# Six packed tiles in place of seven, pruning in nine pieces in place of six, and natural tiles 6 to 11 by column halves from two transposing loads

## Chip, cores, metric

One core of one Trainium2 chip. The metric is the device time of one execution in microseconds (us), median of several; the profile's own span is about 1.8 us shorter than that time. A run is called fast when it lies within 1.5% of the fastest run of the same kernel, otherwise slow. Only fast runs are compared, unless it is said otherwise; a single look has no state of its own.

## The reference

```python
# B, S, D = 16, 512, 1024; all bf16
wg = w.reshape(G, 4, D)                      # 2:4 sparsity along the rows of w
mag = jnp.abs(wg)
thr = ...                                    # second largest magnitude of each four
wp = (wg * (mag >= thr)).reshape(D, D)
return jnp.einsum("bsd,df->bsf", x, wp) + b  # 8192 tokens x 1024 x 1024
```

So: prune the weights, then a dense product of 8192 x 1024 by 1024 x 1024, which is 64 token tiles of 128.

## The kernel before

Pruning compares four rows of w, so w is loaded "packed": the four rows of a group lie side by side in a partition. A few token tiles (the packed tiles, 0 to 6) are multiplied in this packed order, with x transposed on the matrix engine (PE), while the rest of w is still being pruned piece by piece on VectorE. The pruned pieces are also saved to memory and loaded again in natural row order (`reload`). The remaining 57 tiles (natural tiles) use that copy, and x that a transposing load brings in.

```python
NPK = 7                                   # packed tiles
batches: 5, 4, 8, 8, ...                  # natural tiles of one transposing load each
pieces = [(0,0,256), (0,256,512), (1,0,256), (1,256,512), (0,512,1024), (1,512,1024)]
# (row half of w, called group 0 or 1; first column, last column); order of all PE, VectorE and ScalarE work is a fixed list:
#   T6a = transpose x of tile 6, group 0;  F5 = 5 filler matmuls (on zeros, unused);  M5.1 = tile 5 with piece 1;
#   abs/hi/lo/t1/t2/thr/mask/mult + piece = pruning;  C = copy a transpose out;  S = stage;
#   W4 = save piece 4 from ScalarE's queue
...
run(order)
save(0, 0, 256); save(0, 256, 512); save(1, 0, 256); save(1, 256, 512)    # SyncE's queue
load_batch(0)        # transposing load, 5 tiles
reload(0)            # columns 0..511 of the pruned weights, natural order, 1 MB
reload(1)            # columns 512..1023, needs the saves of pieces 4 and 5
load_batch(1)        # transposing load, 4 tiles
load_batch(2)
for t in (2, 0, 3, 1, 6, 5, 4):
    finish(t)        # bias, output store of a packed tile
# first batch of natural tiles: column half 0 of all its tiles, then half 1;
# all later tiles: both halves together
```

## Time and profile before

235.36 us, median of 3 runs (235.29 to 235.66).

| what | value | view |
|---|---|---|
| PE's share of the chain that ended last | 98% | the page, part 4 |
| first packed matmul / first natural matmul | 7.01 / 33.46 us | timeline of PE |
| last product of the pruning (VectorE) | 26.00 us | timeline of VectorE |
| last save landed | 32.15 us | semaphore events of the trace |
| second reload: issued, landed, wanted by PE | 32.22, 38.95, about 42.1 us | the same, and the timeline |

The chain that ended last, by engine and by line. L394 are the natural matmuls of both halves, L359 those by one half, L219 the packed ones, L131 fillers, L194 transposes:

```profile
PE 98%; DVE 0%; issue 0%
PE ps L394 76%; PE ps L219 10%; PE ps L359 9%; PE ps L131 2%; PE tp L194 2%; DVE o L363 0%; DVE zeros L80 0%
```

The last pieces of the same chain in order of time, up to 51 us (start, duration, what). There is no wait in it; packed work (L219) goes straight over into natural work (L359):

```profile
15.63 2.62 PE ps L219 x24
18.25 0.22 PE tp L194 x4
18.48 15.14 PE ps L219 x84
33.62 17.27 PE ps L359 x80
```

SyncE's queue in order of time (start, duration of the issue). The two reloads stand together; the issue of the second waits inside that row for the last save. The next transposing load (L244) comes after both:

```profile
17.45 5.87 SPq L244 DMA_TRANSPOSE xb<-in_x_dram  x1
23.50 9.10 SPq L184 DMA_DIRECT2D wp_nat<-wp_scratch  x2
32.64 25.50 SPq L244 DMA_TRANSPOSE xb<-in_x_dram  x2
```

The transfers (what, queue, count, KB each, us from issue to landing), first for the saves issued between 26 and 27 us, then for the reload issued at 32.2 us:

```profile
wp_scratch<-wp ACTq DMA_DIRECT2D x2, 512.0 KB, 5.2
...
wp_nat<-wp_scratch SPq DMA_DIRECT2D x1, 1024.0 KB, 6.7
```

### The profile page before, as it was taken

How to read it: one execution, taken by the hardware profiler on the slowest of the kernel's cores; microseconds unless marked ns; L12 is line 12 of the kernel's file. 1: busy time of each engine (PE TensorE's matmuls, PEld its weight loads, DVE VectorE, ACT ScalarE, POOL GpSimd, SP SyncE). 2: the span in 40 equal slices, each digit the busy share in tenths (PEclk: the TensorE clock that was granted, in tenths of full speed). 3: DMA queues.
4: the chain of work that ended last, by engine and by line, in shares of the span. 5: the costliest groups of instructions: out<-in, count | busy, mean ns of one | idle time of the engine just before them, and what ended most of it. 6: DMA issues, size and time to landing. Idle time of an engine off the chain costs nothing.

```text
span 233.2 us, 2871 instructions
## 1 busy us (share of the span) xinstructions
PE 229.5 (98%) x1184; PEld 112.8 (48%) x1184; DVE 104.2 (45%) x177; ACT 15.2 (7%) x27; POOL 0.7 (0%) x6
## 2 busy tenths in 40 slices
PE   8999999999999999999999999999999999999995
PEld 5987444444444444444444444444444444444443
DVE  3999559533343244244234334334324424423434
ACT  3679000000000000000000000000000000000000
POOL 1000000000000000000000000000000000000000
PEclk9999999999999999999999999999999999999999
DMA  6999969999999952992239921697221221122122
GB/s 189 297 327 248 322 214 224 282 257 247 241 340 258 273 166 88 209 285 94 90 74 253 257 91 46 146 239 202 90 90 49 88 93 63 72 90 91 47 89 90
DMA packets 79500, 40.29 MB, mean 173 GB/s; under 512 B 60416, under 2 KB 71936, under 8 KB 79488
## 3 DMA queue, kind: packets, MB, share of 16 engines
q1 hardware_dynamic: 68208, 22.32, 43.9%
q10 hardware_dynamic: 11280, 17.80, 22.9%
q8 instruction: 9, 0.15, 0.3%
q14 instruction: 3, 0.02, 0.0%
HBM read 6.29 MB, written 18.87 MB: 108 GB/s over the span
## 4 chain that ended last, share of the span: by engine, by line
PE 98%; DVE 0%; issue 0%
PE ps L394 76%; PE ps L219 10%; PE ps L359 9%; PE ps L131 2%; PE tp L194 2%; DVE o L363 0%; DVE zeros L80 0%
## 5 line engine op out<-in xcount | busy, mean ns | idle before, releaser
L394 PE MATMUL ps<-wp_nat,xb 128*128 128x512 bf16 x816 | 176.3, 379 | 0.0
L394 PEld LDWEIGHTS <-xb 128*128 128x128 bf16 x816 | 79.8, 98 | 96.3
L363 DVE TENSOR_TENSOR o<-ps,bias_sb 128x512 bf16<-128x512 f32 (+1 forms) x116 | 74.0, 677 | 117.2 <-PE ps L394 110.8
L219 PE MATMUL ps<-wp,xt 128*128 128x256 bf16 (+1 forms) x168 | 25.5, 308 | 0.0
L359 PE MATMUL ps<-wp_nat,xb 128*128 128x512 bf16 (+2 forms) x112 | 21.1, 349 | 0.0
L219 PEld LDWEIGHTS <-xt 128*128 128x128 bf16 x168 | 16.2, 98 | 7.5
L359 PEld LDWEIGHTS <-xb 128*128 128x128 bf16 x112 | 10.4, 98 | 10.7
L233 DVE TENSOR_TENSOR o<-ps,bias_sb 128x512 bf16<-128x512 f32 x7 | 4.8, 685 | 5.1 <-PE ps L219 5.1
L131 PE MATMUL ps<-zeros 128*128 128x128 bf16 (+1 forms) x32 | 5.3, 328 | 1.0 <-DVE zeros L80 1.0
L154 ACT ACTIVATE mag<-w_sb 128x1024 bf16<-128x1024 bf16 (+1 forms) x4 | 6.0, 1488 | 1.0 <-DMA w_sb<-in_w_dram 1.0
L151 DVE TENSOR_TENSOR wp<-w_sb,mag 128x1024 bf16<-128x1024 bf16 (+2 forms) x7 | 5.4, 766 | 0.2
L151 DVE TENSOR_TENSOR mag<-mag,hi 128x1024 bf16<-128x1024 bf16 (+2 forms) x7 | 5.3, 767 | 0.2
L199 ACT COPY xt<-tp 128x256 f32<-128x256 f32 x14 | 4.9, 372 | 5.3 <-PE tp L194 5.3
L194 PE MATMUL tp<-ident,x 128*128 128x128 bf16 x56 | 5.0, 227 | 0.0
L234 DVE TENSOR_TENSOR o<-st,bias_sb 128x512 bf16<-128x512 f32 x7 | 4.8, 679 | 0.0
L131 PEld LDWEIGHTS <-zeros 128*128 128x128 bf16 x32 | 3.0, 125 | 2.6 <-issue 1.7
L194 PEld LDWEIGHTS <-x 128*128 128x128 bf16 x56 | 4.0, 117 | 0.4 <-DMA x<-in_x_dram 0.2
L228 ACT COPY st<-ps 128x512 f32<-128x512 f32 x7 | 3.6, 609 | 0.1
L151 DVE TENSOR_TENSOR hi<-mag 128x512 bf16<-128x512 bf16 (+1 forms) x6 | 3.0, 507 | 0.0
L151 DVE TENSOR_TENSOR lo<-mag 128x512 bf16<-128x512 bf16 (+1 forms) x6 | 3.0, 508 | 0.0
L161 DVE TENSOR_SCALAR mag<-w_sb 128x1024 uint16<-128x1024 uint16 x2 | 0.9, 427 | 2.9 <-DMA w_sb<-in_w_dram 2.9
L151 DVE TENSOR_TENSOR hi<-hi,lo 128x256 bf16<-128x256 bf16 (+1 forms) x6 | 2.0, 336 | 0.2
(11 smaller groups left out, 6.4 us busy)
## 6 DMA issues: line engine op xcount, KB each, us to landing
out_dram<-o ACTq DMA_DIRECT2D x58, 256.0 KB, 3.9
wp_nat<-wp_scratch SPq DMA_DIRECT2D x2, 1024.0 KB, 6.4
x<-in_x_dram SPq DMA_DIRECT2D x5, 256.0 KB, 5.0
out_dram<-o ACTq DMA_DIRECT2D x10, 128.0 KB, 1.7
w_sb<-in_w_dram SPq DMA_DIRECT2D x4, 256.0 KB, 4.3
w_sb<-in_w_dram SPq DMA_DIRECT2D x2, 512.0 KB, 7.1
wp_scratch<-wp SPq DMA_DIRECT2D x4, 256.0 KB, 5.6
wp_scratch<-wp ACTq DMA_DIRECT2D x2, 512.0 KB, 5.2
```

Source lines behind the costliest of these rows:

```text
L131: pe(nc.tensor.matmul(warm_ps[:, :rep * P], lhsT=zeros[:], rhs=zeros[:, None, :].to_broadcast([P, rep, P]), start=True, stop=True))
L151: dve(nc.vector.tensor_tensor(out, a, b_, op=op))
L154: act(nc.scalar.activation(self.mag[:], self.w, Act.Abs))
L194: pe(nc.tensor.transpose(tp[:, m, :], xg[:, m, :], ident[:]))
L199: act(nc.scalar.copy(xt[:].bitcast(fp32), xpk[(t, g)][:].bitcast(fp32)))
L219: pe(nc.tensor.matmul(ps[:, c0 - h * FH:c1 - h * FH], lhsT=xpk[(t, g)][m], rhs=wp[:, g, m, c0:c1], start=(new and m == ms.start), stop=(le ...
L228: act(nc.scalar.copy(st[:], ps_open.pop((t, 0))[:]))
L233: dve(nc.vector.tensor_tensor(o[:, FH:], ps_open.pop((t, 1))[:], bias_sb[:, FH:], op=Alu.add))
L234: dve(nc.vector.tensor_tensor(o[:, :FH], staged.pop(t)[:], bias_sb[:, :FH], op=Alu.add))
L359: pe(nc.tensor.matmul(ps, lhsT=xt[:, kt, :], rhs=wp_nat[:, kt, c0:c1], start=(kt == 0), stop=(kt == KT - 1)))
L363: dve(nc.vector.tensor_tensor(o[:, c0:c1], ps, bias_sb[:, c0:c1], op=Alu.add))
L394: pe(nc.tensor.matmul(pss[h][:], lhsT=xt[:, kt, :], rhs=wp_nat[:, kt, h * FH:(h + 1) * FH], start=(kt == 0), stop=(kt == KT - 1)))
```

## The change

Its intent: start the packed matmuls earlier (a first piece of only 128 columns, with its own smaller load), hide VectorE's dependent gaps by interleaving the chains of neighbouring pieces, and save eight transposes with one packed tile fewer. PE then comes to the natural tiles one tile earlier, so six of them (6 to 11) are done by halves, to give the second reload time; their x comes in two loads of three tiles, the second one between the reloads.

```diff
-    NPK = 7
-    ... batches of 5, 4, 8, 8, ...
+    NPK = 6
+    for nb in (3, 3, 4, 8, 8, 8, 8, 8, 8): ...
+    LEAD = 2                                  # batches done by column halves
-    load_w(0, 0, 256)
+    load_w(0, 0, 128)
     ...
+    load_w(0, 128, 256)
     ...                                       # order of the other loads changed too
-    pieces = [(0, 0, 256), (0, 256, 512), (1, 0, 256), (1, 256, 512), (0, 512, 1024), (1, 512, 1024)]
+    pieces = [(0, 0, 128), (0, 128, 256), (0, 256, 512), (1, 0, 256), (1, 256, 512), (0, 512, 768), (0, 768, 1024), (1, 512, 768), (1, 768, 1024)]
     order = { ...                             # new lists for PE, VectorE, ScalarE
+            "T5a F12 T3a T2a F8 M5.0y M3.0y M5.1 M2.1 M2.0y T4a M3.1 M5.0x M2.0x T1a T0a ...
     ...
     load_batch(0)
     reload(0)
+    load_batch(1)
     reload(1)
-    load_batch(1)
     load_batch(2)
-    for t in (2, 0, 3, 1, 6, 5, 4):
+    for t in (3, 2, 1, 0, 4, 5):
         finish(t)
     ...                                       # column halves for all tiles of the first LEAD batches
```

## The prediction

> **What bounds the kernel.** The matrix engine (PE). The chain of waits is 98% PE: 76% in the paired natural matmuls, 9% in natural groups of one column half, 10% in packed matmuls, 2% fillers, 2% transposes. In the timeline PE starts at 0.99 us, never rests over 0.1 us, and ends at 230.5 of 233.2 us. Only PE work and new holes in PE's row can change the time.
>
> **PE work.** Start-to-start steps in the timeline: 216 ns for a 512-column natural matmul, 109 ns for a 256-column packed one, 107 ns for a 128-column filler or transpose until about 5.1 us and 56 ns after it. The Trainium skill, "TensorE: Matmul & The Clock Gate", Part 1, gives the same two steps for a cold and a warm array; this trace agrees.
> - Sixteen column-half matmuls go from packed (2 x 109 ns) to natural (216 ns): about -0.04 us.
> - The 256-column first piece becomes two of 128: estimated 56 ns a matmul instead of 54.5: +0.07 us.
> - Eight transposes fewer, two fillers more. Before, the first packed matmul starts at 7.01 us, behind 20 transposes and 18 fillers. After, it stands behind 12 and 20: I estimate 6.57 us if nothing waits. -0.4 us.
> Net: -0.35 to -0.4 us of 235.36. The change trims only the start.
>
> **Can pruning feed PE that early?** VectorE's rule in the timeline: duration about 0.15 us + 0.53 ns an element; an independent instruction starts 0.08 us before its predecessor ends, a dependent one 0.03 us after. That reproduces the pruning of before to 0.03 us (last product 26.0 us). Applied to the new order: 22 more VectorE instructions, but interleaving hides most dependent gaps. The first load is half the size; I estimate it lands at 3.4 us (before: 3.77), the first product is ready at 6.4, the last at 26.8 us. PE needs nearly each piece just as it comes: I estimate 0 to 0.4 us of holes, typically 0.1, mostly near 7.8 us. Its 256-byte packets won't halve the time: such packets took 18 ns before, 512-byte ones 27.
>
> **The other edge: reloads.** Packed work ends at about 29.7 us instead of 33.5. Before, the first half of the natural weights landed at 29.5 and the second at 38.95, needed at 42.1. After: the first should land near 27 (3 tiles in its transposing load, not 5), good for 29.7. The second waits for the last save (product 26.8, landing 31.5 to 32.5), took 6.7 us before, so lands at 38.3 to 39.8, needed at 40.0 (six tiles by halves buy 10.4 us). Slack falls from 3.1 us to about 1; output stores issued just before it can eat that. Chance of a hole of up to 1 us: a quarter. Later batches keep their slack; steady state and tail are identical.
>
> **Prediction: 235.1 us, range 234.7 to 235.8. Faster by 2%: 0.5%; within 2%: 98.5%; slower: 1%.**
>
> **What would show it.** Right: first packed matmul at 6.5 to 6.8 us, natural matmuls from 29.6 to 30.1, no PE idle at 40 us, VectorE's last product at 26.5 to 27.3. Wrong: PE waiting for the second reload near 40 us, for the first near 30, or for VectorE at 6.5 to 9 us.
>
> **What would make it wrong.** A slow landing of the first small loads; the second reload held by stores and transposing loads; a clock that warms at another moment.

## The result

238.45 us, median of 4 runs (237.91 to 239.52), against 235.32 (235.07 to 235.66) for the kernel before on the same chip. The ratio is 1.0138, 95% interval 1.0099 to 1.0176: slower by 1.4%, and outside the predicted range of 234.7 to 235.8. Ratios here and below are the mean time of one kernel's fast runs over that of the other's in the same rounds, so they are not quite the ratio of the medians quoted. All four runs are fast; the profiled one is the slowest of them (239.52).

The page of the profile after, chain by engine and by line. L404 and L364 are what L394 and L359 were. PE has fallen from 98% to 84%: the pruning, a save and a reload stand in the chain:

```profile
PE 84%; DMA 7%; DVE 6%; issue 1%; ACT 1%; SPq 0%
PE ps L404 74%; PE ps L364 7%; DMA wp_nat<-wp_scratch 4%; DMA wp_scratch<-wp 3%; PE ps L131 2%; DVE hi L151 2%; DVE wp L151 2%; DVE mag L151 1%; DVE lo L151 1%; PE tp L194 1%; PE ps L219 1%; ACT mag L154 0%; ACT xt L199 0%; DVE o L368 0%; DVE zeros L81 0%
```

The same chain in order of time from 26 to 56 us. Read upwards, it says what PE's matmul at 43.25 us had waited for: the second reload, which had waited for the last save, which had waited for VectorE's last product:

```profile
26.77 0.70 DVE wp L151
27.48 0.02 issue
27.50 6.44 DMA wp_scratch<-wp
...
34.00 9.20 DMA wp_nat<-wp_scratch
43.20 0.05 issue
43.25 0.82 PE ps L364 x3
```

PE in order of time. The bracket tells that PE was idle for 2.33 us before the matmul at 43.25 and that the reload ended it. (By starts of matmuls the hole is 2.5 us: the step from 40.54 to 43.25 less one matmul.)

```profile
30.40 10.52 PE L364 MATMUL ps<-wp_nat,xb 128*128 128x512 bf16 x47
43.25 12.22 PE L364 MATMUL ps<-wp_nat,xb 128*128 128x512 bf16 x47 [2.33 <-DMA wp_nat<-wp_scratch]
```

SyncE's queue. The second transposing load now stands between the reloads, and its issue alone takes 8.35 us:

```profile
17.35 3.56 SPq L244 DMA_TRANSPOSE xb<-in_x_dram  x1
21.11 0.43 SPq L184 DMA_DIRECT2D wp_nat<-wp_scratch  x1
21.59 8.35 SPq L244 DMA_TRANSPOSE xb<-in_x_dram  x1
34.00 0.38 SPq L184 DMA_DIRECT2D wp_nat<-wp_scratch  x1
```

The saves issued at 22.1 and 27.5 us, and the second reload, from issue to landing:

```profile
wp_scratch<-wp ACTq DMA_DIRECT2D x1, 512.0 KB, 9.0
...
wp_scratch<-wp ACTq DMA_DIRECT2D x1, 512.0 KB, 6.4
...
wp_nat<-wp_scratch SPq DMA_DIRECT2D x1, 1024.0 KB, 9.2
```

And the granted clock in 40 slices of the span, first row before, second after:

```profile
PEclk9999999999999999999999999999999999999999
...
PEclk9999999799999999999999999999999999999999
```

In the profiled run the clock fell to half for 3.41 us, from 44.43 us, 1.2 us behind the hole. That costs another 1.7 us (3.41 us of matmuls at half speed), and 2.5 + 1.7 = 4.2 us is the distance of this run to the median of before. (Against the profiled run of before, 234.98 us, it is 4.5 us; the remaining 0.3 to 0.4 us is the later start, taken up under e13.) The other three runs, at 237.9 to 238.6 us, had granted clocks of 1.000, 0.999 and 1.000: there the fall of the clock is no part, or next to none, of the loss, and the hole is what remains for nearly all of it. That is argued, as those runs left no trace; e1 tests it. The trace thus names the hole. It doesn't say whether the new start would have been faster without it, nor what made the save and the reload late.

### The profile page after: what moved, and what is told of

It is laid out like the page before. It is cut to its first block, busy times and chain, and to the rows that moved or that the text cites. A ratio compares the mean times of both kernels' runs of the same rounds, so it can differ in the third digit from the quotient of the medians.

```text
span 237.7 us, 2992 instructions
## 1 busy us (share of the span) xinstructions
PE 230.8 (97%) x1223; PEld 117.9 (50%) x1242; DVE 105.7 (44%) x199; ACT 14.3 (6%) x26; POOL 0.7 (0%) x6
## 4 chain that ended last, share of the span: by engine, by line
PE 84%; DMA 7%; DVE 6%; issue 1%; ACT 1%; SPq 0%
PE ps L404 74%; PE ps L364 7%; DMA wp_nat<-wp_scratch 4%; DMA wp_scratch<-wp 3%; PE ps L131 2%; DVE hi L151 2%; DVE wp L151 2%; DVE mag L151 1%; DVE lo L151 1%; PE tp L194 1%; PE ps L219 1%; ACT mag L154 0%; ACT xt L199 0%; DVE o L368 0%; DVE zeros L81 0%
## 5 line engine op out<-in xcount | busy, mean ns | idle before, releaser
L404 PE MATMUL ps<-wp_nat,xb 128*128 128x512 bf16 x799 | 175.4, 379 | 0.9
L368 DVE TENSOR_TENSOR o<-ps,bias_sb 128x512 bf16<-128x512 f32 (+1 forms) x118 | 75.4, 677 | 123.4 <-PE ps L404 108.6
L404 PEld LDWEIGHTS <-xb 128*128 128x128 bf16 x816 | 79.8, 98 | 96.3
L364 PE MATMUL ps<-wp_nat,xb 128*128 128x512 bf16 (+2 forms) x126 | 26.3, 368 | 2.4 <-DMA wp_nat<-wp_scratch 2.3
L219 PE MATMUL ps<-wp,xt 128*128 128x256 bf16 (+1 forms) x216 | 22.0, 261 | 0.0
L364 PEld LDWEIGHTS <-xb 128*128 128x128 bf16 x128 | 12.3, 101 | 16.2 <-DMA wp_nat<-wp_scratch 2.8
L219 PEld LDWEIGHTS <-xt 128*128 128x128 bf16 x216 | 19.1, 98 | 1.8
L154 ACT ACTIVATE mag<-w_sb 128x1024 bf16<-128x1024 bf16 x6 | 6.5, 1078 | 0.0
L233 DVE TENSOR_TENSOR o<-ps,bias_sb 128x512 bf16<-128x512 f32 x6 | 4.1, 686 | 1.8 <-PE ps L219 1.8
L199 ACT COPY xt<-tp 128x256 f32<-128x256 f32 x12 | 4.1, 375 | 6.6 <-PE tp L194 6.6
L151 DVE TENSOR_TENSOR lo<-lo 128x256 bf16<-128x256 bf16 (+1 forms) x9 | 2.4, 269 | 0.0
```

Source lines behind the costliest of these rows:

```text
L151: dve(nc.vector.tensor_tensor(out, a, b_, op=op))
L154: act(nc.scalar.activation(self.mag[:], self.w, Act.Abs))
L199: act(nc.scalar.copy(xt[:].bitcast(fp32), xpk[(t, g)][:].bitcast(fp32)))
L219: pe(nc.tensor.matmul(ps[:, c0 - h * FH:c1 - h * FH], lhsT=xpk[(t, g)][m], rhs=wp[:, g, m, c0:c1], start=(new and m == ms.start), stop=(le ...
L233: dve(nc.vector.tensor_tensor(o[:, FH:], ps_open.pop((t, 1))[:], bias_sb[:, FH:], op=Alu.add))
L364: pe(nc.tensor.matmul(ps, lhsT=xt[:, kt, :], rhs=wp_nat[:, kt, c0:c1], start=(kt == 0), stop=(kt == KT - 1)))
```

## The experiments

Three questions. Is the hole all of the loss (theory T1), or is the new start itself slower (rival R1)? What makes the reload late: the place of the second transposing load (T2), the output stores, or just the later last product? And where is the 0.35 us that the start should have gained? Fourteen runs in four batches (e1 to e4, e5 to e8, e9 to e12, e13 and e14); each batch ran on one chip, beside runs of the kernel before, but the four chips differ. So kernels of different batches are compared by their ratios to before.

| run | what | median us (all) | before in the same rounds | ratio, 95% interval |
|---|---|---|---|---|
| after | the change | 238.45 (4) | 235.32 | 1.0138, 1.0099 to 1.0176 |
| e1 | second reload from the unpruned w, no wait | 235.46 (4) | 235.31 | 1.0003, 0.9984 to 1.0023 |
| e2 | stores held | 236.62 and 237.17 fast, 242.34 and 243.85 slow | 235.31 | 1.0064, 1.0042 to 1.0086 |
| e3 | one load of six tiles, reloads together | 237.34 (4) | 235.31 | 1.0087, 1.0057 to 1.0117 |
| e4 | second reload in two | 235.42, 236.17, 237.47 fast, 241.16 slow | 235.31 | 1.0041, 0.9999 to 1.0083 |
| e5 | last save ahead of the second transposing load | 236.15 (4) | 235.51 | 1.0027, 1.0009 to 1.0045 |
| e6 | *before*, with its second transposing load between the reloads | 244.68 (4) | 235.51 | 1.0381, 1.0354 to 1.0407 |
| e7 | e1 once more | 236.29 (1) | 235.51 | - |
| e8 | e1, first two pieces in one load | 235.51 (4) | 235.51 | 0.9999, 0.9982 to 1.0016 |
| e9 | e1, x of tiles 4, 1, 0 shared | 235.28 (6) | 235.44 | 1.0000, 0.9982 to 1.0019 |
| e10 | e5 with stores held | 235.76 (4) | 235.44 | 1.0014, 0.9997 to 1.0031 |
| e11 | e5, first two pieces in one load | 236.18 (6) | 235.44 | 1.0030, 1.0014 to 1.0045 |
| e12 | second transposing load behind the second reload | 249.82 (1) | 235.44 | - |
| e13 | e1, fillers ahead of the late x | 236.39 (6) | 235.63 | 1.0036, 1.0011 to 1.0061 |
| e14 | e10, fillers ahead of the late x | 235.84 (6) | 235.63 | 1.0006, 0.9988 to 1.0024 |

e1, e7, e8, e9 and e13 give wrong results on purpose; all others are correct.

### e1: the hole taken away

```diff
+    w_nat = w.rearrange("(kt p) f -> p kt f", p=P)
     def reload(h):
         fs = slice(h * FH, (h + 1) * FH)
-        sp(nc.sync.dma_start(wp_nat[:, :, fs], scr_nat[:, :, fs]))
+        src = w_nat if h == 1 else scr_nat
+        sp(nc.sync.dma_start(wp_nat[:, :, fs], src[:, :, fs]))
```

> The changed kernel, with one edit: the second column half of the natural weights is loaded from the unpruned w in memory, not from the saved pruned copy, so this load no longer waits for the last save (the result is wrong on purpose). Theory T1, the late second reload: all of the loss is the hole in PE's row near 41 us that ends with this reload, and the clock that drops behind it. Then no PE idle there, the time falls from 238.4 to 234.7 to 235.4 us, and the start gains 0.1 to 0.4 us over before. Rival R1, the new start (nine pieces, smaller VectorE instructions, a clock that warms later) is itself slower and the hole only absorbs it: then the hole closes but the time stays at 236 us or more, with PE gaps before 30 us.

The hole is gone; PE runs from the first natural tile through all twelve groups of halves without a bracket (96 matmuls, two of whose records are missing):

```profile
30.66 20.88 PE L367 MATMUL ps<-wp_nat,xb 128*128 128x512 bf16 x94
```

The ratio falls from 1.0138 to 1.0003. So T1 holds for the loss: without the wait for the late reload the change costs nothing that these rounds resolve. But it also gains nothing: the 0.1 to 0.4 us that I expected on top did not show. R1, as a loss of a microsecond, is refuted; as a gain that stayed away, it is a second failed step, taken up below.

### e2, e3, e4: three ways to bring the reload forward

e2 holds the packed tiles' stores:

```diff
-        issue("act", of[t * P:(t + 1) * P, :], o[:])
+        held.append((t, o))
     ...
+    act(nc.scalar.copy(spark[:, 1:2], wp_nat[:, KT - 1, Dout - 1:Dout]))   # waits for the reload
+    for t, o in held:
+        issue("act", of[t * P:(t + 1) * P, :], o[:])
```

with 16 output buffers in place of 10.

> The changed kernel, with the six output stores of the packed tiles held back until the second reload has landed (ScalarE reads one element of it first), and 16 output buffers in place of 10. T1 says that two things delay the reload: its last save lands at 33.9 us (before: 32.2), and its packets then wait behind the stores of three or four finished tiles (first reload packets 1.3 us after the issue at 34.0, 9.2 us to landing, before 6.7). If the stores are the larger part: landing in about 6.7 us, at 40.5 to 41, hole 0 to 0.5 us, time 235.2 to 236. If the stores are not a cause: hole about 2.3 us as now and time about 238.4.

Two of four runs were slow, the profiled one among them, so only times count: the fast two are 236.62 and 237.17. The loss falls to about half. Stores are then a part of the cause, not all of it; e10 comes back to them. (In the slow profiled run PE waited 0.2 us for the second reload, but 3.6 us at 70 us for a later transposing load. Nothing is concluded from a slow run.)

e3 puts the six tiles' x into one load:

```diff
-    for nb in (3, 3, 4, 8, 8, 8, 8, 8, 8):
+    for nb in (6, 4, 8, 8, 8, 8, 8, 8):
-    LEAD = 2
+    LEAD = 1
     reload(0)
-    load_batch(1)
     reload(1)
+    load_batch(1)
```

> The changed kernel with one of its parts undone: natural tiles 6 to 11 come in one transposing load ahead of the first reload, and both reloads stand together, as before; the columns halves and the start stay. T1 with the second transposing load (3 tiles, in flight from 26.5 to 32 us) as what delays the last saves: the last save lands at 31.5 to 32.5, not 33.9, the second reload at 38.5 to 39.5, in time; but the first reload is pushed back by the three more tiles, to about 30.5, where PE needs it at 30.4, so a hole of 0 to 1 us near 30.5. Time 235 to 236.2. If the second transposing load is not the cause the last save still lands near 34 and the time stays at 238.

The hole went to the other reload, and it was larger than I had allowed. The first reload was issued 4 us later than in the changed kernel and landed at 32.50 us; PE wanted it at about 30.8:

```profile
32.64 20.88 PE L364 MATMUL ps<-wp_nat,xb 128*128 128x512 bf16 x94 [1.64 <-DMA wp_nat<-wp_scratch]
```

The last save landed at 33.86 us, no earlier than in the changed kernel (33.94), against my expectation: now the first reload (landed at 32.50) was still in flight beside it. The second reload took 6.76 us and landed at 40.69. That would have been in time even for a PE that was not late (30.8 + 10.4 = 41.2 us, an estimate). The run says that three more tiles in front of the first reload are too many; it does not tell T2 from its rivals.

e4 cuts the second reload by row groups, so that only half of it waits for the last save:

```diff
-    def reload(h):
+    def reload(h, k0=0, k1=KT):
         ... wp_nat[:, k0:k1, fs] from scr_nat[:, k0:k1, fs] ...
-    reload(1)
+    reload(1, 0, 4)
+    reload(1, 4, 8)
```

> The changed kernel with the second reload cut in two: the rows of group 0 (pieces 5 and 6, saved earlier) in one load, those of group 1 in another that alone waits for the last save. T1: the part that waits for the last save is half as large, so it lands about 1.5 us sooner after the save, and PE needs it 0.86 us later, so the hole of 2.3 us falls to 0 to 0.8 us and the time to 235.2 to 236.4. R1: no change in time, 238.4.

Fast runs of 235.42, 236.17 and 237.47 us: on the mean the loss falls from 1.38% to 0.41%, as expected, but with an unusual scatter (and a slow run of 241.16). The slow run is the profiled one; PE waited in it not for the second reload but, at 55 us, 2.7 us for a later transposing load. The cure aims at the right place and isn't a stable one.

### e5, e6, e12: where the second transposing load stands

e5 lets SyncE issue the last save ahead of that load:

```diff
             "S1 S0 abs8 W6 W8"
->           "S1 S0 abs8 W6"
     reload(0)
+    save(*wsave[8])
     load_batch(1)
     reload(1)
```

> The changed kernel with one edit: the last save (group 1, columns 512 to 1023) is issued by SyncE ahead of the second transposing load, in place of by ScalarE behind it. In the changed kernel's trace the save issued at 22.1 us moved no packet until 27.5, as long as the second transposing load (issued 21.6 to 29.9) stood ahead of it with its packets not yet begun; before, with no such load in between, saves issued at 26.0 began 1.5 us later. Theory T2: it is the place of the second transposing load, ahead of the last saves, that makes them and so the second reload late. Then the first save starts within 2 us of its issue and lands at 27 to 29 us (31.2 now), the last at 31 to 32.5 (33.9 now), the second reload at 38.5 to 41 (43.2), hole 0 to 0.5 us near 41, perhaps up to 0.7 us near 36 for the second load's tiles; time 235.3 to 236.3. If it's plainly too much traffic and not the order, the last save lands near 34 again and the time stays above 237.

The last save now landed at 31.98 us, 3.9 us after its issue (6.4 in the changed kernel), and the second reload at 41.16. No hole was left at 41 us; PE waited 0.2 us for x near 36. The last save, the second reload, and PE's only wait for natural work up to 60 us (in total, times, longest):

```profile
wp_scratch<-wp SPq DMA_DIRECT2D x1, 512.0 KB, 3.9
...
wp_nat<-wp_scratch SPq DMA_DIRECT2D x1, 1024.0 KB, 7.9
...
PE ps L365 <- DMA xb<-in_x_dram: 0.2, 1, 0.2
```

The time is 236.15, ratio 1.0027. So the loss shrank to a fifth. One expectation failed and corrects T2: the *other* save (issued at 22.73 us) did not start within 2 us of its issue. Its first packet moved at 27.2 us, although no transposing load was ahead of it any more.

e6 does the reverse: the kernel of before, with this one line of the change.

```diff
     reload(0)
-    reload(1)
     load_batch(1)
+    reload(1)
     load_batch(2)
```

> The kernel of before with one part of the change alone: its second transposing load (4 tiles) goes ahead of the second reload. T2: the last saves (issued at 26.0 and 26.6) now stand behind that load and land at 34 to 36 us in place of 32.2, the second reload at 41 to 44 in place of 38.95; PE needs it at 42.1, so a hole of 0 to 2 us near 42 and 235.3 to 238 us. If the order does no harm: last save at 32 to 33, no hole, 235.3 as before.

It costs far more than I had expected, 3.8%. Not all of that is PE's wait: in the profiled run the matmuls just behind it ran at half clock (up to 53.5 us, about 1.4 us of loss, an estimate), and all four runs had a granted clock of 0.985 or 0.986. First the saves (before: 5.2 us), then the wait:

```profile
wp_scratch<-wp ACTq DMA_DIRECT2D x2, 512.0 KB, 14.8
```

```profile
50.67 2.32 PE L359 MATMUL ps<-wp_nat,xb 128*128 128x512 bf16 x5 [8.18 <-DMA wp_nat<-wp_scratch]
```

Four tiles and two saves were in flight together from about 31 to 40.5 us. The windows view gives what the DMA engines moved then (last number, GB/s; the one before it is the engines' busy share), followed by the same view of *before* for a stretch with transposing packets almost alone (19.7 to 24.7) and one with saves almost alone (28.5 to 30.5), and of the changed kernel for its overlap (28 to 32):

```profile
31.00:40.50 9.50, 9.45 (x45) 4.31 (x44) 7.90 (x14) 0.00 (x0) 0.00 (x0) 1.00 1.22 209
```

```profile
19.70:24.70 5.00, 5.00 (x33) 3.05 (x32) 4.86 (x8) 3.04 (x7) 0.00 (x0) 1.00 1.22 268
28.50:30.50 2.00, 2.00 (x11) 0.94 (x10) 1.27 (x2) 0.00 (x0) 0.00 (x0) 1.00 1.07 376
```

```profile
28.00:32.00 4.00, 3.95 (x31) 2.92 (x30) 2.69 (x5) 0.00 (x0) 0.00 (x0) 1.00 1.21 282
```

The Trainium skill's page "DMA: Bandwidth & Descriptors", section "Issuing engines are not separate DMA queues", says that DMAs issued by different engines run on the same 16 DMA engines and interleave. The trace agrees: in the last window the two queues moved 0.60 and 0.53 MB. Saves that ran almost alone at 376 GB/s thus got about 132 (0.53 MB in 4 us) beside the transposing load, and in e6 the total fell to 209.

e12 is the counter-test in the changed kernel:

```diff
     reload(0)
-    load_batch(1)
     reload(1)
+    load_batch(1)
     load_batch(2)
```

> The changed kernel with its second transposing load behind the second reload (the order that before has). It shows the trade: nothing is in the saves' way, so the last save lands at 31 to 32.5 us and the second reload at 38 to 40, in time; but natural tile 9, whose x is in that load, is wanted at about 35.6 and comes at 41 to 44. PE hole of 5 to 8 us near 36, time 240 to 244.

The saves and the second reload:

```profile
wp_scratch<-wp ACTq DMA_DIRECT2D x1, 512.0 KB, 7.2
...
wp_scratch<-wp ACTq DMA_DIRECT2D x1, 512.0 KB, 3.2
...
wp_nat<-wp_scratch SPq DMA_DIRECT2D x1, 1024.0 KB, 6.7
```

With nothing in its way the last save landed at 30.80 us instead of 33.94, and the second reload at 37.60 instead of 43.20. (Another chip, but the same position up to there: the first reload landed at 28.05 us here and at 28.06 in the changed kernel, the last save was issued at 27.61 and 27.50.) But natural tile 9 waited for its x:

```profile
47.14 13.06 PE L364 MATMUL ps<-wp_nat,xb 128*128 128x512 bf16 x47 [11.29 <-DMA xb<-in_x_dram]
```

It is one look, of unknown state, but 11.3 us are beyond doubt. The two-load arrangement needs the second load early, and early is where it collides with the saves. Here too the first of the two saves, issued at 22.24, moved its first packet at 26.6 us. Only the first reload was ahead of it, so its late start is not the transposing load's work.

### e10: what the stores cost

e5 with e2's edit.

> The kernel with the last save ahead of the second transposing load, and also the packed tiles' output stores held until the second reload has landed (16 output buffers). It asks what the stores cost the reload, with the transposing load out of the way. If they share its time: landing 5 to 6.5 us after the issue, in place of 7.9. No PE hole at 41 us in either, so the time should be the same within 0.5 us, or up to 2 us longer if the delayed stores push a later transposing load past its need (as with the stores held before, where PE waited 3.6 us at 70 us).

The reload took 6.0 us; in e5, with the stores free to go, 7.9:

```profile
wp_nat<-wp_scratch SPq DMA_DIRECT2D x1, 1024.0 KB, 6.0
```

It landed at 38.66 us, and PE had no hole through all twelve groups of halves:

```profile
30.56 20.88 PE L370 MATMUL ps<-wp_nat,xb 128*128 128x512 bf16 x96
```

The ratio is 1.0014, an interval that includes 1: level with before. So the stores seem to lengthen the reload (e5 ran on another chip, so the 1.9 us are only roughly their share). The bytes that ScalarE's queue moved between the reload's issue and its landing point the same way: 1.27 MB in the changed kernel (9.2 us) and 1.19 in e5 (7.9), but 0.32 in e3 (6.76), 0.27 in e12 (6.7), 0.03 before (6.7) and none in e10 (6.0). My picture of how they do it, in e2's expectation, is not borne out: the reload's first packet moved 1.4 us after its issue in the changed kernel (35.4 us) and 1.2 us after it here (33.9), so the stores ahead of it do not hold back its start. The time goes while its packets are moving.

### e7 to e9, e11, e13, e14: the gain that stayed away

e7 is e1 once more (its label suggests otherwise). e8 adds one load for the first two pieces:

```diff
-    load_w(0, 0, 128)
+    load_w(0, 0, 256)
     ...
-    load_w(0, 128, 256)
```

> The same kernel as the one with the unpruned second reload, looked at a second time beside its variant below (wrong result on purpose): PE should again wait 0.3 to 1.3 us in all for the packed tiles' x loads between 5 and 16 us, and begin the natural tiles at 30.2 to 30.9 us.

> The kernel with the unpruned second reload (no hole there; wrong result on purpose), and the first two column pieces of w loaded by one load of 256 columns, as before, though still pruned as two. It isolates the new start. In the five traces of the new start [...]the x loads behind them landed 0.6 us or more later than I had put them, so that PE waited for x and ScalarE's first absolute values (hence all later products, 27.5 to 28.1 us at the last) came later. If these loads are the cause: first load at 3.8 us, first packed matmul 0.2 to 0.3 us later, but no x waits above 0.2 us, last product at 27.0 to 27.4, natural tiles from 29.9 to 30.3 us; time 0.1 to 0.5 us under its twin with two loads. If not: x waits as before and no gain.

PE's holes before 31 us, summed over the steps from one matmul's start to the next, are 0.8 us in e7 and 1.0 in e8 (in e1: 0.7); natural tiles begin at 31.32 and 30.75. e8's ratio is 0.9999 where e1's was 1.0003, and intervals of 0.4% overlap: the two small first loads are not shown to cost anything. In e8 the x of tiles 1 and 0 still landed at 8.56 us, no earlier than in the changed kernel (8.54), so my reason (the 256-byte packets) isn't shown either.

e9 takes two x loads away:

```diff
-    load_x(4, 5, 0)
-    load_x(0, 2, 0)
+    x_sb[(4, 0)] = x_sb[(5, 0)]
+    x_sb[(0, 0)], x_sb[(1, 0)] = x_sb[(2, 0)], x_sb[(3, 0)]
```

> The kernel with the unpruned second reload (no hole there), and in it the first-group x of packed tiles 4, 1 and 0 is taken from that of tiles 5, 3 and 2, so their two loads fall away (384 KB less between 5 and 9 us; wrong result on purpose). The arithmetic and its order stay. It asks where the predicted gain of the start (0.35 us) went. If into waits for these x loads and what hangs on them (ScalarE's first absolute values stand behind the copies of tiles 1 and 0): PE holes before 31 us fall from 0.7 to 1.8 us to at most 0.4, the last product from 27.5 to 28.1 to 26.7 to 27.2, natural tiles begin at 29.6 to 30.2, and the time is 234.7 to 235.1, that is 0.3 to 0.7 us under before of the same rounds. If the start's own work is longer than I summed: time as before (235.3 to 235.6) although the waits are gone.

The later x waits vanished, the last product came at 27.11 and the natural tiles began at 30.02 us, as the first reading had it. But the first wait was still there, and so was the time: ratio 1.0000. The line of the list of waits (who waited for what; us in total, times, longest):

```profile
PE tp L197 <- DMA x<-in_x_dram: 0.6, 1, 0.6
```

This was the wait for the x of tiles 3 and 2 (landed at 6.02 us; 5.58 in the changed kernel), with eight fillers still to come behind it. e13 therefore moves the fillers ahead of it:

```diff
-            "T5a F12 T3a T2a F8 M5.0y M3.0y M5.1 M2.1 M2.0y T4a M3.1 ...
+            "T5a F20 T3a T2a M5.0y M5.1 M3.0y M2.1 M2.0y T4a M3.1 ...
```

> The kernel with the unpruned second reload (no hole; wrong result on purpose), its eight fillers between the transposes of tiles 3 and 2 and the first packed matmul moved ahead of those transposes, and one packed matmul group of tile 5 moved up. PE work is the same. If the missing gain of the start went into fillers that stand behind a late x load: first packed matmul at 6.5 to 7.0 us whatever the load does, time 0.1 to 0.4 us under before of the same rounds (ratio 0.998 to 0.9995). If it went elsewhere: ratio 1.000 or more.

A miss: ratio 1.0036, slower. The first packed matmul came at 6.71 us, as wished. But PE met the next loads that had not landed: x of tiles 3 and 2, then of tiles 1 and 0, for group 1. What it had gained it waited for there:

```profile
10.99 0.64 PE L197 MATMUL tp<-ident,x 128*128 128x128 bf16 x8 [0.31 <-DMA x<-in_x_dram]
16.26 0.64 PE L197 MATMUL tp<-ident,x 128*128 128x128 bf16 x8 [0.69 <-DMA x<-in_x_dram]
```

e11 (e5 with one first load) and e14 (e10 with the fillers moved) are the corresponding correct versions.

> The best mended version of the change, correct: last save ahead of the second transposing load, and the first two pieces of w in one load. The two edits alone gave 236.15 (from 238.4) and no clear difference. Expected 235.4 to 236.2: no hole near 41 us, and 0 to 0.5 us at 36 us, PE holes of 0.4 to 1.2 us before 17 us. It beats before only if the x loads happen to land on time; I give that one chance in five.

> The best correct version so far (last save ahead of the second transposing load, stores held, 16 output buffers; ratio 1.0014) with the same move of fillers. Expected ratio 0.9985 to 1.001, that is equal to before within what the rounds resolve; no PE hole near 41 us, and at most 0.3 us near 36.

Neither beats before (1.0030 and 1.0006), and nothing here points to a version that would.

The loads, over these traces: the x of tiles 1 and 0 for group 1, the last x that the new start needs, landed at 14.10 us before and at 13.97 in e6, which has the start of before. With the new start it landed at 14.72 in the changed kernel, at 14.11 (e12) and 14.15 (e11), and as late as 15.88 (e5) and 16.21 (e13); e1 and e7, the same kernel, have 15.30 and 15.95. And the start of the natural tiles: 33.46 before, which less the 3.47 us of one packed tile's matmuls (16 of 256 columns at 109 ns and 8 of 512 at 216) would be 29.99 with six packed tiles; measured with six, their x loads all there and no other wait in between, 30.33 (e11) to 31.58 us (e13). So in the profiled runs the new start is later than the old one, not earlier.

Waits for x are only a part of the reason. The other is the moment at which the matmul clock becomes full, which the prediction named as a risk: 5.13 us before, 6.88 in the changed kernel, and 4.24 (e3) to 7.01 (e7) over the traces that record it (e13's doesn't). Until then a 128-column matmul takes 107 ns instead of 56. In the changed kernel's run this cost 0.8 us more than before, and PE waited for no x at all: its holes up to 30.4 us sum to less than 0.1 us. In e10 the clock was full at 4.58 us and the holes are 1.3 us. Slow steps and holes taken off, what is left is the work itself: the natural tiles would begin at 27.5 us in each of the thirteen traces with the new start that record the clock, and at 31.1 before. That is 3.6 us apart, and 3.46 of it are the 16 natural matmuls that stand in for the packed tile. So the new start's own work is only about 0.2 us shorter: an estimate from the step times of these traces. Why the input loads mostly land later, though fewer bytes are asked for, is not settled.

## Why the prediction was wrong

- *What bounds the kernel* was right: PE at 98%, and a hole in PE's row is paid in full. e1 is the proof from the other side: take the hole away and 1.0138 becomes 1.0003.
- *PE work* (-0.35 to -0.4 us): no run shows the gain. With the hole gone the change equals before (1.0003, 0.9999, 1.0000). The intervals are as wide as the gain, so times can't settle the sum; the traces put it at about -0.2 us (end of the last section). One term that I left out: the packed matmuls of 512 columns become two of 256 each (2 x 109 ns instead of 216, 48 times: +0.1 us). And the profiles show the holes that I had put at 0 to 0.4 us: 0.7 in e1, 0.8 in e7, 1.0 in e8.
- *Can pruning feed PE* was a little off: last product at 27.46 us in the changed kernel and 27.1 to 28.4 in the variants, where I had 26.8 (and up to 27.3 as right). In the changed kernel 0.45 us of that is one wait of VectorE, at 10.88 us, for ScalarE's first absolute values. These stand behind the copies of tiles 1 and 0, which wait for PE's transposes. In this run PE reached these transposes at 8.82 us without a wait, just after their x had landed (8.54): the late full clock held it up here, not the load. In other runs it was the load (e5: PE waited 0.5 us for x here).
- *The other edge: reloads* is the step that failed. The mechanism was named and given one chance in four and a hole of up to 1 us; it was in fact the whole result, within what the rounds of e1 resolve, with a hole of 2.3 to 2.5 us. Two terms were too small. The last save landed at 33.94 us, not at 31.5 to 32.5: by e12, which is one look, 3.1 us of that are the transposing load ahead of it and beside it (30.80 without). The reload then took 9.2 us, not 6.7: by e12 (6.7) and e10 (6.0) that is 2.5 us longer than with a free path, and what the stores of finished tiles moved beside it (1.27 MB, against 0.27 and none) fits that, though the share of each is not separated. Together: 43.20 us, where e12 has 37.60 and I had 38.3 to 39.8. I had taken 6.7 us over from a place where almost nothing else was moving (0.03 MB on ScalarE's queue).
- Adding up the bytes would have warned me. Between 27.7 us, when the first packet of the saves moved, and the landing of the reload, the new order puts two saves (1.05 MB), three tiles of x (0.79), three stores (0.79) and the reload (1.05) on the same engines: 3.7 MB, an estimate from the sizes in the profile. At 376 GB/s, the rate of the saves almost alone, that's 9.8 us; at 282, the rate of the mixture, 13.0. That gives 37.5 to 40.7 us, before any latency, for a reload wanted at 40: no slack left, though not yet the hole. In the trace it was more: 4.4 MB at 286 GB/s between 27.7 and 43.2 us, as the stores had moved 1.5 MB and not 0.79.
- *A falling clock behind the hole* was not in the prediction at all: 1.7 us in one of four runs. The clock that warms at another moment was, and happened in the profiled run (6.88 us against 5.13); it moved the start, not the result.
- The first reload, good for 29.7 by my count, landed at 28.06 us (I had 27). That edge held.

What stays open: how much the earlier first matmul is worth by itself, as the rounds resolve 0.4%; why the input loads mostly land later with the new start; why a save waits for what another queue was given before it (the order is shown at the end, not its reason).

## What to carry to other kernels

When a change shortens the compute between a write to memory and the use of what is read back, the slack of that round trip is the first thing to price: add up all bytes that stand on the DMA engines between the write's issue and the reload's landing, also of other queues, and don't take over a duration that was measured where the DMA engines had almost nothing else to do. Moving one load in the queue cost 3.8% in a kernel that was otherwise untouched, a clock that fell behind the wait included. And in these traces an earlier first matmul was used up by the waits for the next input loads (e13).

## What the Trainium skill lacked or had wrong

- "TensorE: Matmul & The Clock Gate", section "Why this matters for your kernels", advises no PE idle gaps over about 3 us between bursts of matmuls. In the profiled run of the changed kernel a hole of 2.3 to 2.5 us was followed by 3.41 us at half clock; in its three other fast runs the granted clock was 1.000, 0.999 and 1.000. So a gap under that figure was no sure protection. The length of the low stretch, 3.41 us, agrees with the window of Part 1 of that page.
- "DMA: Bandwidth & Descriptors", section "Queues, rings and completion order", says that each DMA engine goes round robin between the queue rows it has work for. In the changed kernel the save issued on ScalarE's queue at 22.12 us moved no packet until 27.7 us, while SyncE's queue was busy with the first reload; from 22.5 to 27.5 us the list of queues has one line only, below. It was the same with no transposing load ahead (e12: issued 22.24, first packet 26.6). For trn2 the page doesn't say when work issued on one queue can be held so long by another. In the traces of before, the changed kernel, e3, e6 and e12 the saves and loads issued between 20 and 28 us began to move in the order of their issue over both queues. In the changed kernel the reload issued at 21.11 moved from 22.2 us, the transposing load of 21.59 from 26.8 and the save of 22.12 from 27.7; in e6 the transposing load of 24.49 moved from 28.4 and the save of 26.40 from 30.9; in e3 the save of 22.57 was issued before the first reload (25.28) and moved before it (26.5 and 27.9).

```profile
q1 hardware_dynamic: 1372, 1.11, 90.1%
```

- The same page's section "DMA Transpose (X-bar)" gives no rate for a transposing load next to ordinary transfers. Here: 268 GB/s almost alone, 376 for saves almost alone, 282 for both in the changed kernel, 209 over 9.5 us in e6.
- No page has an account of how input loads slow each other at a kernel's start; here the same x landed at 13.97 and 14.10 us in two traces with the old start, and between 14.1 and 16.2 with the new one (13.4 in e9, which has two loads fewer).
